# A channel gate over 113 MB: 18 tiles of 64 rows instead of 12 rows and 19 tiles of 60

## The chip, the cores and the metric

One core of one Trainium2 chip. The metric is device time in microseconds (us) of one execution; the profile's span is about 1.4 us shorter than it.

## The reference, cut to what matters

```python
x: (1, 384, 384, 384) bf16, w1d: (1,)
g = jnp.einsum("bhwc->bc", x) / (H * W)      # mean of each channel over all pixels
s = sigmoid(g * w1d[0])                      # one gate per channel
return x * s[:, None, None, :]
```

As 128 partitions see it, x is 1,152 rows of 384 channels per partition. Strictly, everything must be read before anything can be multiplied.

## The kernel before

It reads and writes everything once. It takes a gate `s_early` from the first 4 rows, multiplies by it at once, sums all rows meanwhile, and at the end compares the true gate, in bf16, with the early one. Only if they differ does a second pass run over everything.

The 1,152 rows are a small first tile of 12 and 19 tiles of 60, in four slots of an SBUF arena. For each tile: the load; sums of 44 rows by TensorE (matmuls with ones) and of 16 by VectorE (`reduce_sum`); the gate in place on VectorE; the store. A slot's next load waits for its store to land.

```python
FIRST, EARLY, TILE, SLOTS, BOTH, FORE, OWN = 12, 4, 60, 4, 3, 32, 16
...
    LEAD = EARLY + 4
    load(base, FIRST, 0, hi=LEAD)                       # 8 rows ahead, SyncE's queue
    plan.dma("sync", w_one[0:1, 0:1], w1d.unsqueeze(0), writes=["w_one"])
    for k in range(SLOTS):                              # tiles 0 to 2: half on each queue
        load(slot(k), TILE, row0(k), ("sync", "scalar") if k < BOTH else ("sync",))
        if k == 0:
            load(base, FIRST, 0, ("scalar",), lo=LEAD)  # the other 4 rows
...
    for k in range(n_tiles):                            # steady state
        if k >= SLOTS:
            for i in range(2) if k == SLOTS else () if k < SLOTS + 2 else (k - SLOTS,):
                sum_own(i)                              # VectorE: reduce 16 rows, add
                put(slot(i), TILE, row0(i), ...)        # VectorE: gate; ScalarE: issue store
            if k == SLOTS:
                pause(slot(k))                          # 3 us on ScalarE before load 4
            load(slot(k), TILE, row0(k), ...)
...
    put(slot(last), TILE, row0(last), slot(n_tiles))    # the end
    sum_own(last)
    put(base, FIRST, 0)
    join_own()                                          # VectorE's sums, through TensorE
    add_banks(1, copy=False)                            # TensorE's sums, then the check
```

Of the kernel before, what the change touches and what calls it, by code (L numbers as in the profile page):

```python
# [3 lines left out]
P = 128  # L4
ROW = 384
BF16 = mybir.dt.bfloat16
# [4 lines left out]
ALU = mybir.AluOpType  # L11
# [143 lines left out]
WIDE = 512  # L155



FIRST, EARLY, TILE, SLOTS, BOTH, FORE, OWN = 12, 4, 60, 4, 3, 32, 16


PAUSE = 9


def bass_standalone__channel_attn_eca__vision_kernel(
# [5 lines left out]
    B, H, W, C = x.shape  # L171
# [12 lines left out]
    wrong = nc.alloc_sbuf_tensor("wrong", [P, 1], F32)  # L184
    redo = nc.alloc_sbuf_tensor("redo", [P, 1], I32)
    total = nc.alloc_sbuf_tensor("total", [P, C], F32)
    own = nc.alloc_sbuf_tensor("own", [P, C], F32)
    part = nc.alloc_sbuf_tensor("part", [P, C], F32)
    terms = nc.alloc_sbuf_tensor("terms", [P, 3 * C], BF16)
# [9 lines left out]
    def at(r0, n):  # L199
        assert r0 + n <= n_arena  # L200
        return arena[:, r0 * C : (r0 + n) * C]

    def rows(r0, n):
        return [("sb", r) for r in range(r0, r0 + n)]
# [3 lines left out]
        v, to_v = (at(r, n).rearrange("p (t c) -> p t c", t=n) for r in (place, to))  # L208
        return lambda e: e.tensor_tensor(to_v, v, s_b, ALU.mult)  # L209

    n_tiles = (n_rows - FIRST) // TILE
    base = SLOTS * TILE
    assert (n_rows - FIRST) % TILE == 0 and base + FIRST + 1 + PAUSE <= n_arena
    assert FIRST % 4 == EARLY % 4 == (TILE - OWN) % 4 == 0 and EARLY + 4 < FIRST
    last = n_tiles - 1
    ready = nc.alloc_semaphore("ready")

    def slot(k):
        return k % SLOTS * TILE

    def row0(k):
        return FIRST + k * TILE


    s_true = at(base + FIRST, 1)
    plan = Planner(nc, "a", 70)

    def load(place, n, r0, queues=("sync",), lo=0, hi=None, reads=()):

        i, hi = lo, hi or n  # L230
        for queue, m in zip(queues, split(hi - lo, -(-(hi - lo) // len(queues)))):
            plan.dma(
                queue,
                at(place + i, m),
                dram(x_rows, r0, n)[:, i * C : (i + m) * C],
                reads=reads,
                writes=rows(place + i, m),
            )
            i += m
# [19 lines left out]
    def add_rows(e, group, column, n, start, stop):  # L259

        n_wide = n * C // WIDE
        all_of = [
            mm(
                e,
                acc[group][i % 3][:, :],
                ones[:],
                arena[:, column + i * WIDE : column + (i + 1) * WIDE],
                start and i < 3,
                stop and i >= n_wide - 3,
            )  # L270
            for i in range(n_wide)
        ]
        return all_of[-1]

    def sum_first():
        plan.op(
            "tensor",
            lambda e: add_rows(e, 0, base * C, EARLY, True, True),
            reads=["ones"] + rows(base, EARLY),
            writes=["acc0"],  # L280
        )

    def sum_others():

        def one(e, s):
            e.wait_ge(ready, 1).then_inc(ready, -1)  # L286
            for r, n in ((0, FORE), (FORE, TILE - OWN - FORE)):
                add_rows(e, 1, (slot(s) + r) * C, n, False, False).then_inc(
                    plan.sems["tensor"], 1
                )  # L290

        def emit(e):
            add_rows(e, 1, (base + EARLY) * C, 4, True, False)
            rounds = -(-n_tiles // SLOTS)
            some = n_tiles - (rounds - 1) * SLOTS
            with e.Fori(0, rounds) as k:
                for s in range(some):
                    one(e, s)
                if some < SLOTS:
                    with e.If(k < rounds - 1):  # L300
                        for s in range(some, SLOTS):
                            one(e, s)
            add_rows(
                e, 1, (base + EARLY + 4) * C, FIRST - EARLY - 4, False, True
            ).then_inc(plan.sems["tensor"], 1)

        plan.streams["tensor"].append(("block", emit, None))

# [34 lines left out]
    def join_own():  # L343

        for i in range(3):
            term = terms[:, i * C : (i + 1) * C]
            plan.op(
                "vector",
                lambda e, term=term: e.tensor_copy(term, own[:]),  # L349
                reads=["own"],  # L350
                writes=[f"term{i}"],
            )
            if i < 2:
                plan.op(
                    "vector",
                    lambda e, term=term: e.tensor_tensor(  # L356
                        own[:], own[:], term, ALU.subtract
                    ),
                    reads=["own", f"term{i}"],
                    writes=["own"],  # L360
                )
        for i in range(3):
            term = terms[:, i * C : (i + 1) * C]
            plan.op(
                "tensor",
                lambda e, i=i, term=term: mm(
                    e, acc_own[:, :C], ones[:], term, i == 0, i == 2
                ),
                reads=["ones", f"term{i}"],
                writes=["acc_own"],  # L370
            )
        plan.op(
            "vector",
            lambda e: e.tensor_tensor(total[:], total[:], acc_own[:, :C], ALU.add),  # L374
            reads=["acc_own", "total"],
            writes=["total"],
        )

    def put(place, n, r0, to=None, parts=None):
        to, i = place if to is None else to, 0  # L380
        for m in parts or [n]:
            plan.op(
                "vector",
                gate(to + i, place + i, m, s_early),
                reads=["s_early"] + rows(place + i, m),
                writes=rows(to + i, m),
            )
            i += m
        plan.final.append(
            plan.dma("scalar", dram(o_rows, r0, n), at(to, n), reads=rows(to, n))  # L390
        )

    def pause(r0):

        to = at(base + FIRST + 1, PAUSE)
        plan.op(
            "scalar",
            lambda e: e.activation(  # L398
                to, warm[:, 0:1].broadcast_to([P, PAUSE * C]), ACT_F.Sigmoid
            ),  # L400
            reads=["warm"],
            writes=rows(r0, 1) + ["pause"],
        )
# [26 lines left out]

    plan.op("gpsimd", lambda e: e.memset(warm[:, 0:1], 0.0), writes=["warm"])
    plan.op("vector", lambda e: e.memset(ones[:], 1.0), writes=["ones"])  # L432
    LEAD = EARLY + 4
    load(base, FIRST, 0, hi=LEAD)
    plan.dma("sync", w_one[0:1, 0:1], w1d.unsqueeze(0), writes=["w_one"])
    for k in range(SLOTS):
        load(slot(k), TILE, row0(k), ("sync", "scalar") if k < BOTH else ("sync",))
        if k == 0:
            load(base, FIRST, 0, ("scalar",), lo=LEAD)
    heads = {e: len(plan.streams[e]) for e in ("sync", "scalar")}  # L440
    weight()
    sum_first()
    add_banks(0, copy=True)
    plan.op(
        "scalar",
# [3 lines left out]
        reads=["total", "w_scaled0", "warm1"],  # L449
        writes=["s_early"],  # L450
    )
    plan.need("tensor", rows(base, LEAD))
    sum_others()

    for k in range(n_tiles):
        if k >= SLOTS:

            for i in range(2) if k == SLOTS else () if k < SLOTS + 2 else (k - SLOTS,):
                sum_own(i)
                put(slot(i), TILE, row0(i), parts=None if i else (FORE, TILE - FORE))  # L460
            if k == SLOTS:
                pause(slot(k))
            load(slot(k), TILE, row0(k), reads=["pause"] if k == SLOTS else ())
        there = rows(slot(k), TILE) + (rows(base + LEAD, FIRST - LEAD) if k == 1 else [])
        plan.relay(ready, "gpsimd", "tensor", there, rows(slot(k), FORE), ["acc1"])
        plan.signals("tensor", rows(slot(k) + FORE, TILE - OWN - FORE), ["acc1"])
    plan.signals("tensor", rows(base, FIRST), ["acc1"])
    for k in range(n_tiles - SLOTS, last):
        sum_own(k)
        put(slot(k), TILE, row0(k))  # L470

    put(slot(last), TILE, row0(last), slot(n_tiles))
    sum_own(last)
    put(base, FIRST, 0)
    join_own()


    add_banks(1, copy=False)
    plan.op(
        "scalar",  # L480
        lambda e: e.activation(  # L481
            s_true, total[:], ACT_F.Sigmoid, scale=w_scaled[:, 1:2]
        ),
        reads=["total", "w_scaled1"],
        writes=["s_true"],
    )
    plan.op(
        "vector",
# [19 lines left out]


    again = Planner(nc, "b", 30)  # L510
    half, r0 = base // 2, 0
    for k, n in enumerate(split(n_rows, half)):
        place = k % 2 * half
        again.dma("sync", at(place, n), dram(x_rows, r0, n), writes=rows(place, n))
        again.op(
            "vector",
            gate(place, place, n, s_true),
            reads=rows(place, n),
            writes=rows(place, n),
        )  # L520
        again.final.append(
            again.dma("scalar", dram(o_rows, r0, n), at(place, n), reads=rows(place, n))
        )
        r0 += n
# [93 lines left out]
```

## Time and profile before

| | before |
|---|---|
| median of 6 runs (lowest to highest) | 528.07 us (527.95 to 528.75) |
| span of the profiled run | 526.7 us |
| share of 16 DMA engines' span, both queues | 99.7% |
| VectorE busy | 451 us (86%) |
| TensorE busy | 178 us (34%) |

How to read it: the shares are of one span, so the fullest resource bounds the kernel unless the chain of waits says otherwise. The prediction below goes through both. One thing is added here: three lines of the timeline of the start, with start, duration, engine, operation and, in brackets, the idle time before it with what ended it (ACTq is a transfer that ScalarE issues).

```profile
18.66 9.48 PE L247 MATMUL acc<-arena,ones 128*128 128x512 bf16 x33 [6.64 <-PEq L286]
...
38.57 23.45 ACTq L109 DMA_DIRECT2D out_dram<-arena  x2
...
74.23 3.08 ACT L398 ACTIVATE arena<-warm 128x3456 bf16<-128x3456 f32 x1 [60.11 <-DMA out_dram<-arena]
```

Tile 0's sums start at 18.7 us, the first store is issued at 38.6 (the second at 61.7, in the same merged line), and the first store has landed at 74.2, when the pause begins.

### The profile page before, as it was taken

How to read it: one execution, taken by the hardware profiler on the slowest of the kernel's cores; microseconds unless marked ns; L12 is line 12 of the kernel's file. 1: busy time of each engine (PE TensorE's matmuls, PEld its weight loads, DVE VectorE, ACT ScalarE, POOL GpSimd, SP SyncE). 2: the span in 40 equal slices, each digit the busy share in tenths (PEclk: the TensorE clock that was granted, in tenths of full speed). 3: DMA queues.
4: the chain of work that ended last, by engine and by line, in shares of the span. 5: the costliest groups of instructions: out<-in, count | busy, mean ns of one | idle time of the engine just before them, and what ended most of it. 6: DMA issues, size and time to landing. Idle time of an engine off the chain costs nothing.

```text
span 526.7 us, 905 instructions
## 1 busy us (share of the span) xinstructions
PE 178.2 (34%) x640; PEld 0.2 (0%) x2; DVE 451.1 (86%) x82; ACT 5.8 (1%) x5; POOL 0.3 (0%) x5
## 2 busy tenths in 40 slices
PE   2534660060606051414233241515060606060701
PEld 0000000000000000000000000000000000000000
DVE  1899999999796969796969696979697979889796
ACT  1000020000000000000000000000000000000000
POOL 0000000000000000000000000000000000000000
PEclk9978877576766767675858585858585858576765
DMA  9999999999999999999999999999999999999998
GB/s 387 430 422 460 406 448 395 444 448 448 395 444 448 448 395 444 448 441 402 444 448 434 409 445 444 434 413 441 448 430 416 441 444 434 416 441 444 430 420 367
DMA packets 6340, 226.51 MB, mean 430 GB/s; under 512 B 706, under 2 KB 706, under 8 KB 962
## 3 DMA queue, kind: packets, MB, share of 16 engines
q10 hardware_dynamic: 3456, 122.49, 53.8%
q1 hardware_dynamic: 2882, 104.01, 45.9%
q14 instruction: 2, 0.02, 0.0%
HBM read 113.25 MB, written 113.25 MB: 430 GB/s over the span
## 4 chain that ended last, share of the span: by engine, by line
DMA 64%; DVE 27%; issue 4%; PE 2%; ACT 0%; DVEq 0%
DMA out_dram<-arena 33%; DMA arena<-in_x_dram 31%; DVE arena L209 13%; DVE part L331 12%; PE acc L247 1%; DVE own L338 1%; DVE total L319 0%; DVE own L356 0%; DVE terms L349 0%; ACT arena L481 0%; DVE total L489 0%; DVE total L374 0%; DVE wrong L497 0%; PE acc_own L247 0%; DVE redo L503 0%
## 5 line engine op out<-in xcount | busy, mean ns | idle before, releaser
L247 PE MATMUL acc<-arena,ones 128*128 128x512 bf16 x635 | 176.3, 447 | 314.0 <-PEq L286 314.0
L209 DVE TENSOR_TENSOR arena<-arena,s_early 128x23040 bf16<-128x23040 bf16 (+3 forms) x21 | 233.5, 11123 | 5.2 <-DMA arena<-in_x_dram 4.0
L331 DVE TENSOR_REDUCE part<-arena 128x384 f32<-128x6144 bf16 x18 | 189.5, 10526 | 53.4 <-DMA arena<-in_x_dram 53.4
L331 DVE TENSOR_REDUCE own<-arena 128x384 f32<-128x6144 bf16 x1 | 10.5, 10495 | 1.1 <-DMA arena<-in_x_dram 1.1
L338 DVE TENSOR_TENSOR own<-own,part 128x384 f32<-128x384 f32 x18 | 10.0, 558 | 0.6
L247 PE MATMUL acc_own<-terms,ones 128*128 128x384 bf16 x3 | 1.4, 478 | 16.8 <-DVE terms L349 16.8
L424 DVE TENSOR_SCALAR w_scaled<-w_all 128x1 f32<-128x1 f32 x2 | 0.2, 152 | 7.9 <-PE w_all L415 7.9
L481 ACT ACTIVATE arena<-total,w_scaled 128x384 bf16<-128x384 f32 x1 | 0.6, 614 | 444.3 <-DVE total L319 444.3
L319 DVE TENSOR_TENSOR total<-total,acc 128x128 f32<-128x128 f32 (+2 forms) x11 | 4.5, 408 | 0.4
L398 ACT ACTIVATE arena<-warm 128x3456 bf16<-128x3456 f32 x1 | 3.1, 3082 | 60.1 <-DMA out_dram<-arena 60.1
L415 PE MATMUL w_all<-w_one,ones 1*128 1x1 bf16 x1 | 0.2, 159 | 9.2 <-DMA w_one<-in_w1d_dram 9.2
L317 DVE COPY total<-acc 128x384 f32<-128x384 f32 x1 | 0.6, 558 | 1.2 <-PE acc L247 1.2
L409 ACT ACT_TABLE_LOAD x1 | 1.3, 1283 | 2.8 <-issue 2.8
L432 DVE MEMSET ones<- 128x128 bf16 x1 | 0.2, 165 | 1.3 <-PEq L603 1.3
L356 DVE TENSOR_TENSOR own<-own,terms 128x384 f32<-128x384 f32 x2 | 1.1, 559 | 0.1
L489 DVE TENSOR_TENSOR total<-arena,s_early 128x384 f32<-128x384 uint16 x1 | 0.6, 559 | 0.7 <-ACT arena L481 0.7
L349 DVE CAST terms<-own 128x384 bf16<-128x384 f32 x3 | 1.1, 357 | 0.1
L374 DVE TENSOR_TENSOR total<-total,acc_own 128x384 f32<-128x384 f32 x1 | 0.6, 556 | 0.6 <-PE acc_own L247 0.6
L446 ACT ACTIVATE s_early<-total,w_scaled 128x384 bf16<-128x384 f32 x1 | 0.6, 614 | 9.2 <-DVE total L319 9.2
L245 PE MATMUL acc<-arena,ones 128*128 128x512 bf16 x1 | 0.6, 608 | 0.0
L497 DVE TENSOR_REDUCE wrong<-total 128x1 f32<-128x384 f32 x1 | 0.6, 553 | 0.0
L409 ACT ACTIVATE warm<-warm 128x1 f32<-128x1 f32 x1 | 0.2, 202 | 0.0
(8 smaller groups left out, 0.9 us busy)
## 6 DMA issues: line engine op xcount, KB each, us to landing
out_dram<-arena ACTq DMA_DIRECT2D x19, 5760.0 KB, 44.7
arena<-in_x_dram SPq DMA_DIRECT2D x16, 5760.0 KB, 40.9
arena<-in_x_dram ACTq DMA_DIRECT2D x3, 2880.0 KB, 34.5
arena<-in_x_dram SPq DMA_DIRECT2D x3, 2880.0 KB, 29.0
out_dram<-arena ACTq DMA_DIRECT2D x1, 1152.0 KB, 11.1
arena<-in_x_dram SPq DMA_DIRECT2D x1, 768.0 KB, 7.7
arena<-in_x_dram ACTq DMA_DIRECT2D x1, 384.0 KB, 21.2
w_one<-in_w1d_dram SPq DMA_DIRECT2D x1, 0.0 KB
```

The costliest lines, as they stand in the source:

```text
L209: return lambda e: e.tensor_tensor(to_v, v, s_b, ALU.mult)
L245: loaded.append(e.matmul(bank, weights, moving, start=start, stop=stop))
L247: return e.add_instruction(mybir.InstMatmult(name=nc.get_next_instruction_name(), engine=mybir.EngineType.PE, ins=[e.lower_ap(moving), e.l ...
L317: emit = lambda e, part=part, of=of: e.tensor_copy(part, of)
L319: emit = lambda e, part=part, of=of: e.tensor_tensor(part, part, of, ALU.add)
L331: lambda e: e.reduce_sum(to[:], view, axis=mybir.AxisListType.X),
L338: lambda e: e.tensor_tensor(own[:], own[:], part[:], ALU.add),
L349: lambda e, term=term: e.tensor_copy(term, own[:]),
L356: lambda e, term=term: e.tensor_tensor(own[:], own[:], term, ALU.subtract),
L374: lambda e: e.tensor_tensor(total[:], total[:], acc_own[:, :C], ALU.add),
L398: lambda e: e.activation(to, warm[:, 0:1].broadcast_to([P, PAUSE * C]), ACT_F.Sigmoid),
L409: lambda e: e.activation(warm[:, 1:2], warm[:, 0:1], ACT_F.Sigmoid),
```

## The change

The intent: no small first tile, fewer and larger transfers, nothing left to gate after the last tile, and a last addition that waits less for TensorE. The first 8 rows of tile 0 are loaded ahead and the early gate comes from its first 4. Since the tiles are larger, the loads of the start are dealt out anew: tile 1 whole on SyncE's queue, tile 2 on ScalarE's.

```diff
-FIRST, EARLY, TILE, SLOTS, BOTH, FORE, OWN = 12, 4, 60, 4, 3, 32, 16
+TILE, SLOTS, EARLY, LEAD, FORE, OWN = 64, 4, 4, 8, 32, 16
...
-    load(base, FIRST, 0, hi=LEAD)
+    load(0, TILE, 0, hi=LEAD)
     plan.dma("sync", w_one[0:1, 0:1], w1d.unsqueeze(0), writes=["w_one"])
-    for k in range(SLOTS):
-        load(slot(k), TILE, row0(k), ("sync", "scalar") if k < BOTH else ("sync",))
-        if k == 0:
-            load(base, FIRST, 0, ("scalar",), lo=LEAD)
+    load(0, TILE, 0, ("sync", "scalar"), lo=LEAD)
+    load(slot(1), TILE, row0(1))
+
+    load(slot(2), TILE, row0(2), ("scalar", "scalar"))
+    load(slot(3), TILE, row0(3))
...
     put(slot(last), TILE, row0(last), slot(n_tiles))
     sum_own(last)
-    put(base, FIRST, 0)
     join_own()                  # without its last addition
-    add_banks(1, copy=False)
+    add_banks(1, copy=True)
+    ... total += acc_own        # the addition, now after the banks
```

Cut: TensorE's sums open and close with matmuls over a column of zeros, since no small tile is there to do it; the true gate goes to a row of the last slot; the second pass has smaller pieces.

More of the change, by code (lines that the diff above doesn't have):

```diff
@@ L186, in bass_standalone__channel_attn_eca__vision_kernel @@
     total = nc.alloc_sbuf_tensor("total", [P, C], F32)
+    zeros = nc.alloc_sbuf_tensor("zeros", [P, 2], BF16)
     own = nc.alloc_sbuf_tensor("own", [P, C], F32)
@@ L209, in gate @@
         return lambda e: e.tensor_tensor(to_v, v, s_b, ALU.mult)
-    n_tiles = (n_rows - FIRST) // TILE
+    n_tiles = n_rows // TILE
     base = SLOTS * TILE
-    assert (n_rows - FIRST) % TILE == 0 and base + FIRST + 1 + PAUSE <= n_arena
-    assert FIRST % 4 == EARLY % 4 == (TILE - OWN) % 4 == 0 and EARLY + 4 < FIRST
+    assert n_rows % TILE == 0 and base + PAUSE <= n_arena
+    assert EARLY % 4 == FORE % 4 == (TILE - OWN) % 4 == 0 and EARLY <= LEAD <= FORE
     last = n_tiles - 1
@@ L221, in row0 @@
     def row0(k):
-        return FIRST + k * TILE
-    s_true = at(base + FIRST, 1)
+        return k * TILE
+    s_true = at(slot(last), 1)
     plan = Planner(nc, "a", 70)
@@ L273, in add_rows, with sum_early, nothing, sum_all @@
         return all_of[-1]
-    def sum_first():
+    def sum_early():
         plan.op(
             "tensor",
-            lambda e: add_rows(e, 0, base * C, EARLY, True, True),
-            reads=["ones"] + rows(base, EARLY),
+            lambda e: add_rows(e, 0, 0, EARLY, True, True),
+            reads=["ones"] + rows(0, EARLY),
             writes=["acc0"],
         )
-    def sum_others():
+    def nothing(e, bank, start):
+        none = zeros[:, 0:1].broadcast_to([P, WIDE])
+        return mm(e, acc[1][bank][:, :], ones[:], none, start, not start)
+    def sum_all():
         def one(e, s):
@@ L292, in emit @@
         def emit(e):
-            add_rows(e, 1, (base + EARLY) * C, 4, True, False)
+            for i in range(3):
+                nothing(e, i, True)
             rounds = -(-n_tiles // SLOTS)
@@ L302, in emit @@
                             one(e, s)
-            add_rows(
-                e, 1, (base + EARLY + 4) * C, FIRST - EARLY - 4, False, True
-            ).then_inc(plan.sems["tensor"], 1)
+            for i in range(3):
+                done = nothing(e, i, False)
+            done.then_inc(plan.sems["tensor"], 1)
         plan.streams["tensor"].append(("block", emit, None))
@@ L371, in join_own @@
             )
-        plan.op(
-            "vector",
-            lambda e: e.tensor_tensor(total[:], total[:], acc_own[:, :C], ALU.add),
-            reads=["acc_own", "total"],
-            writes=["total"],
-        )
     def put(place, n, r0, to=None, parts=None):
@@ L393, in pause @@
     def pause(r0):
-        to = at(base + FIRST + 1, PAUSE)
+        to = at(base, PAUSE)
         plan.op(
@@ L432, in bass_standalone__channel_attn_eca__vision_kernel @@
     plan.op("vector", lambda e: e.memset(ones[:], 1.0), writes=["ones"])
-    LEAD = EARLY + 4
-    load(base, FIRST, 0, hi=LEAD)
+    plan.op("gpsimd", lambda e: e.memset(zeros[:], 0.0), writes=["zeros"])
+    load(0, TILE, 0, hi=LEAD)
     plan.dma("sync", w_one[0:1, 0:1], w1d.unsqueeze(0), writes=["w_one"])
-    for k in range(SLOTS):
-        load(slot(k), TILE, row0(k), ("sync", "scalar") if k < BOTH else ("sync",))
-        if k == 0:
-            load(base, FIRST, 0, ("scalar",), lo=LEAD)
+    load(0, TILE, 0, ("sync", "scalar"), lo=LEAD)
+    load(slot(1), TILE, row0(1))
+    load(slot(2), TILE, row0(2), ("scalar", "scalar"))
+    load(slot(3), TILE, row0(3))
     heads = {e: len(plan.streams[e]) for e in ("sync", "scalar")}
     weight()
-    sum_first()
+    sum_early()
     add_banks(0, copy=True)
@@ L451, in bass_standalone__channel_attn_eca__vision_kernel @@
     )
-    plan.need("tensor", rows(base, LEAD))
-    sum_others()
+    plan.need("tensor", ["zeros"])
+    sum_all()
     for k in range(n_tiles):
@@ L463, in bass_standalone__channel_attn_eca__vision_kernel @@
             load(slot(k), TILE, row0(k), reads=["pause"] if k == SLOTS else ())
-        there = rows(slot(k), TILE) + (rows(base + LEAD, FIRST - LEAD) if k == 1 else [])
+        there = rows(slot(k), TILE)
         plan.relay(ready, "gpsimd", "tensor", there, rows(slot(k), FORE), ["acc1"])
         plan.signals("tensor", rows(slot(k) + FORE, TILE - OWN - FORE), ["acc1"])
-    plan.signals("tensor", rows(base, FIRST), ["acc1"])
+    plan.signals("tensor", [], ["acc1"])
     for k in range(n_tiles - SLOTS, last):
@@ L473, in bass_standalone__channel_attn_eca__vision_kernel @@
     sum_own(last)
-    put(base, FIRST, 0)
     join_own()
-    add_banks(1, copy=False)
+    add_banks(1, copy=True)
+    plan.op(
+        "vector",
+        lambda e: e.tensor_tensor(total[:], total[:], acc_own[:, :C], ALU.add),
+        reads=["acc_own", "total"],
+        writes=["total"],
+    )
     plan.op(
@@ L484, in bass_standalone__channel_attn_eca__vision_kernel @@
         reads=["total", "w_scaled1"],
-        writes=["s_true"],
+        writes=["s_true"] + rows(slot(last), 1),
     )
@@ L510, in bass_standalone__channel_attn_eca__vision_kernel @@
     again = Planner(nc, "b", 30)
-    half, r0 = base // 2, 0
+    above = slot(last) + 1
+    half, r0 = (base - above) // 2, 0
     for k, n in enumerate(split(n_rows, half)):
-        place = k % 2 * half
+        place = above + k % 2 * half
         again.dma("sync", at(place, n), dram(x_rows, r0, n), writes=rows(place, n))
```

## The prediction

> **What bounds the kernel now.** I read the engines' busy line first, then the DMA slices and queues. VectorE looks like the bound (86%), so the reader has to hold it against the DMA engines before believing it.
>
> ```profile
> PE 178.2 (34%) x640; PEld 0.2 (0%) x2; DVE 451.1 (86%) x82; ACT 5.8 (1%) x5; POOL 0.3 (0%) x5
> ...
> DMA  9999999999999999999999999999999999999998
> ...
> DMA packets 6340, 226.51 MB, mean 430 GB/s; under 512 B 706, under 2 KB 706, under 8 KB 962
> ## 3 DMA queue, kind: packets, MB, share of 16 engines
> q10 hardware_dynamic: 3456, 122.49, 53.8%
> q1 hardware_dynamic: 2882, 104.01, 45.9%
> ```
>
> The two queues' packets fill 53.8 + 45.9 = 99.7% of what 16 engines have in the span of 526.7 us, so 525 us each: no hole worth the name. q1 is SyncE's queue (loads), q10 ScalarE's (stores and some early loads). The GB/s line jumps between 395 and 460, but the busy line does not follow it down: packets are long (next part) and I take the dips for the way whole packets are counted into slices, not for lost time. That is a choice of mine.
>
> Next the chain of waits, because a chain that goes through every buffer could also set the pace.
>
> ```profile
> 404.47 44.67 DMA out_dram<-arena
> ...
> 449.15 40.79 DMA arena<-in_x_dram
> ...
> 489.97 12.16 DVE arena L209
> 502.13 10.34 DVE part L331
> ...
> 513.05 2.47 DVE arena L209
> ...
> 523.48 0.15 DVE redo L503
> ```
>
> A slot's life is load 40.8 + reduce, add and gate 23.2 + store 44.7 us, 109 us for four slots, so 27.2 us a tile. But a tile is 2 x 5.9 MB, and at 433 GB/s (what the stretch from 120 to 485 us moves) that is 27.2 us of transfer as well. So the chain is long because transfers queue: a load alone would need 5.9 MB / 433 GB/s = 13.6 us, not 40.8. VectorE has 23.2 us of work per 27.2 us. The bound is the transfer of 226.5 MB; the chain's length is its consequence.
>
> Last, the two ends, where a change of tiling could act:
>
> ```profile
> core 0: us, PE busy (x) PEld busy (x) DVE busy (x) ACT busy (x) POOL busy (x), PEclk, DMA share, GB/s
> 120.00:485.00 365.00, 118.26 (x429) 0.00 (x0) 311.87 (x40) 0.00 (x0) 0.00 (x0) 0.69 1.00 433
> ...
> 515.00:525.30 10.30, 1.43 (x3) 0.00 (x0) 6.97 (x16) 0.61 (x1) 0.00 (x0) 0.50 0.93 401
> 525.30:526.70 1.40, 0.00 (x0) 0.00 (x0) 0.00 (x0) 0.00 (x0) 0.00 (x0) 0.50 0.09 39
> ```
>
> In the packet records the first big packet starts at 1.0 us and the last ends at 526.3 us. What is not transfer is about 1 us of start and 1 us of engines finishing unevenly. The check of the gate ends at 523.6 us (the last line of the chain) and its flag is read by 524.5 us, before the last store lands: it is hidden by 2 us.
>
> **What the Trainium skill says.** "DMA: Bandwidth & Descriptors", section "Specifications", puts the ceiling of 16 engines at 435 GB/s and a core's HBM share at about 358. This trace agrees with the first (433 in the steady stretch, read and write together) and goes over the second, so no HBM limit shows here. The same page, "Queues, rings and completion order", says that an engine goes round-robin between queues packet by packet. The trace agrees: with 23,040-byte packets on both queues each has about 8 of the 16 engines at 22 to 26 us; when SyncE's are 23,040 and ScalarE's 3,072 bytes (14 to 20 us), SyncE's has over 13. I use this for the start. The same page, "Latency and other measured facts", warns of row pitches in HBM of large powers of two, where a copy fell to half rate and a few KiB of padding restored it. A pitch of 64 rows is 48 KB, three times a power of two, where 60 rows are 45 KB; no run so far shows whether that matters.
>
> **The change part by part.**
>
> 1. Bytes: 113.25 MB in and 113.25 MB out, unchanged.
>
> 2. Packets. One packet is one partition's contiguous piece: 46,080 bytes take 1.702 us and 23,040 bytes 0.855 us (medians of the packet records). The difference gives 0.0368 us per 1,000 bytes and 1.702 - 2 x 0.847 = 0.008 us fixed per packet. Before: 5,632 data packets. After: 128 x (7 in the initial loads + 14 later loads + 18 stores) = 4,992. Saved 640 x 0.008 / 16 = **0.3 us**. A 49,152-byte packet should take 0.008 + 1.807 = 1.815 us.
>
> 3. VectorE. Removed: one reduce (10.5), one add (0.6), the 12-row gate's 2.6 us; gates grow by 64/60 in all but cover the same rows. So 451 - 12 = about 439 us busy. None of it is on the bound: 24.1 us of work per tile against 2 x 6.29 MB / 433 GB/s = 29.05 us. Worth 0.
>
> 4. TensorE. 36 matmuls a tile instead of 33 (the last group before has 36 and takes 9.9 us), under the 10.5 us reduce beside it. The six matmuls over a column of zeros only open and close the sums. Worth 0.
>
> 5. The end. After the last load: gate 12.15 x 64/60 = 13.0, reduce and add 10.9, splitting into terms 2.2, banks 2.8 (the matmuls of the terms now run beside them), last add, sigmoid, compare and flag 2.6 + 0.9: 32.4 us against 34.5 before. The 12-row gate's 2.5 us and a wait of 0.5 go, 0.8 comes. Stores still outstanding when the last load lands: the end of the last but two, then two whole tiles of 14.5 us each at one queue's full rate (8 x 1.815), so at least 29 us plus up to one more tile. The last store is issued 13 us after the last load, while the one before it still has work: no hole. By part 6 the phase leaves some 39 us of stores, over 32.4. Worth 0: the check was and stays hidden.
>
> 6. The start, where the order of loads really changes. Per engine each load is 8 packets. Before: tile 1 is split over both queues; after: it is whole on SyncE's queue with 49,152-byte packets, and tile 2 is on ScalarE's with 24,576. Alternating packets from the trace's sizes: the 8 rows ahead land near 7.5 us as now; tile 0's halves (21,504 bytes, 0.80 us) at about 13 and 21 us (before: 14.6 and 18.7, as ScalarE's tiny 4-row packets let SyncE's half run ahead; they are gone). So TensorE's sums of tile 0's first 32 rows end near 28.5 us instead of 26.2, and the first store goes out near 41.4 instead of 38.6. Tile 1 (8 pairs of 1.815 + 0.911) lands near 43 instead of about 30; VectorE then idles 2 us and issues the store of tile 1 near 67 (before 62.0). ScalarE's loads end at 51, SyncE's last initial load near 69; the first store lands near 75 (+1.8 of latency; the same arithmetic for the kernel before gives 72.4 against a measured 74.2). Then only the store of tile 1 has packets until the load of tile 4 arrives after the pause, near 79. It was issued 8 us before it is needed, so the engines stay full. **Worth 0**, but the margin falls from 12 us to 8.
>
> 7. The end's raggedness is that of 16 engines with equal work; packets of 1.8 us at the end instead of 0.35 could add up to 0.5 us.
>
> Sum: -0.3 from packets, +0.2 for raggedness, 0 elsewhere: 528.05 - 0.1 to -0.3, I say **527.8 us**.
>
> **The rivals.**
>
> A. *The check at the end comes out.* If the reader takes the chain at its word, VectorE ends it, and 34.5 - 32.4 = 2 us less after the last load would give 526. Against: the last packets end at 526.3, 2 us after the flag is read. I give it little.
>
> B. *A hole opens at the start.* Tile 1 lands 13 us later, and if the two queues share otherwise than packet by packet, the store of tile 1 misses the end of the first store while the next load still sits behind the pause. Each us of miss is a us of all 16 engines: 2 to 5 us, so 530 to 533. For it: that is the only stretch with a single store at work (70 to 80 us in the trace). Against: the 8 us margin.
>
> C. *The 48 KB pitch slows transfers.* One per cent longer packets cost 5.2 us. For it: only the page's warning. Against: at 45 KB the rate is already the engines' own.
>
> D. *Larger tiles take away a periodic loss.* If the GB/s dips were real, 19 rounds becoming 18 might win 1 to 2%. Against: the 99.7%.
>
> **Range and chances.** Three runs of the kernel before spread over 0.7 us. A and D pull down by 1 to 3 us, B and C up by 2 to 5, each unlikely: 526.3 to 529.6. Two per cent are 10.6 us, which none of A or B reaches: faster 0.01, within 2% 0.96, slower 0.03 (C).
>
> **What would show it.** The two queues should still fill over 99.4% of 16 engines; 49,152-byte packets should take 1.81 to 1.82 us (C: more); the slices from 60 to 90 us should stay at full DMA share (B: a slice under 0.9); VectorE's busy time should fall to about 439 us with no gain in time; the flag should be read at least 2 us before the last store lands. The prediction is wrong if the DMA share has a hole, or if the profile shows the packets themselves changed.

## The result, and the profile after

| | before | after |
|---|---|---|
| median of 6 runs each | 528.07 us | 527.96 us |
| lowest to highest | 527.95 to 528.75 | 527.94 to 528.25 |
| span of the profiled run | 526.7 us | 526.5 us |
| data packets | 5,632 | 4,992 |
| packet time per DMA engine (packet records) | 524.7 us | 524.6 us |
| last packet ends | 526.3 us | 525.9 us |

The ratio is 0.9996, 95% interval 0.9983 to 1.0009: the same. Ratios here are the mean time of one kernel's fast runs over that of the other's of the same rounds, so not quite the ratio of the medians quoted.

The page of the changed kernel, the lines that answer to those in the prediction:

```profile
PE 180.0 (34%) x648; PEld 0.2 (0%) x2; DVE 440.0 (84%) x78; ACT 5.8 (1%) x5; POOL 0.3 (0%) x6
...
DMA packets 5620, 226.51 MB, mean 430 GB/s; under 512 B 626, under 2 KB 626, under 8 KB 754
...
q10 hardware_dynamic: 3024, 122.29, 53.7%
q1 hardware_dynamic: 2594, 104.20, 46.0%
```

VectorE lost 11 us of work and the time did not follow. The queues still fill 99.7% of 16 engines, with the same bytes at the same mean rate.

The end, in the chain of waits (start, duration, what):

```profile
489.92 12.96 DVE arena L210
502.88 10.34 DVE part L338
...
521.28 0.15 DVE redo L510
```

The last load lands at the same time as before (489.9 us), the check is done 2.2 us earlier (before: 523.5 + 0.15), and the stores go on to 525.9: the earlier check has nothing to give.

The start, in the timeline:

```profile
22.77 10.78 PE L248 MATMUL acc<-arena,ones 128*128 128x512 bf16 x36 [10.66 <-PEq L292]
...
44.14 24.76 ACTq L109 DMA_DIRECT2D out_dram<-arena  x2
...
76.09 3.08 ACT L399 ACTIVATE arena<-warm 128x3456 bf16<-128x3456 f32 x1 [61.87 <-DMA out_dram<-arena]
```

The first store is issued 5.6 us later than before, the store of tile 1 at 68.6 us (before 61.7), and yet the first store lands only 1.9 us later. Did the engines stay full? Here are two windows of the changed kernel, of 5 and of 16 us. The columns are window and length, busy time and instructions of TensorE, its weight loads, VectorE, ScalarE and GpSimd, the granted clock, the DMA share and GB/s.

```profile
70.00:75.00 5.00, 2.72 (x7) 0.00 (x0) 5.00 (x1) 0.00 (x0) 0.00 (x0) 0.50 0.79 344
...
66.00:82.00 16.00, 9.67 (x35) 0.00 (x0) 15.97 (x4) 3.08 (x1) 0.00 (x0) 0.68 1.02 442
```

The first line looks like a hole. It is none: in the packet records 16.0 of 16 engines are at work in every 2 us from 70 to 82 us. Whole packets of 1.8 us are counted into windows, and neighbouring windows show 1.09. The second line, long against a packet, is the one to believe.

### The profile page after: what moved, and what is told of

Read it like the earlier page. It is cut to its first block, busy times and chain, and to the rows that moved or that the text cites. A ratio compares the mean times of both kernels' runs of the same rounds, so it can differ in the third digit from the quotient of the medians.

```text
span 526.5 us, 902 instructions
## 1 busy us (share of the span) xinstructions
PE 180.0 (34%) x648; PEld 0.2 (0%) x2; DVE 440.0 (84%) x78; ACT 5.8 (1%) x5; POOL 0.3 (0%) x6
## 4 chain that ended last, share of the span: by engine, by line
DMA 42%; another core or an unknown queue 27%; DVE 21%; issue 7%; SPq 0%; ACT 0%; DVEq 0%
DMA arena<-in_x_dram 24%; DMA out_dram<-arena 18%; DVE part L338 12%; DVE arena L210 7%; DVE own L345 1%; DVE total L326 0%; SPq L109 0%; DVE own L363 0%; DVE terms L356 0%; ACT arena L488 0%; DVE total L496 0%; DVE total L482 0%; DVE wrong L504 0%; DVE total L324 0%
## 5 line engine op out<-in xcount | busy, mean ns | idle before, releaser
L210 DVE TENSOR_TENSOR arena<-arena,s_early 128x24576 bf16<-128x24576 bf16 (+1 forms) x19 | 233.2, 12278 | 11.5 <-PE acc L248 6.5
L338 DVE TENSOR_REDUCE part<-arena 128x384 f32<-128x6144 bf16 x17 | 179.2, 10539 | 56.9 <-DMA arena<-in_x_dram 56.9
L338 DVE TENSOR_REDUCE own<-arena 128x384 f32<-128x6144 bf16 x1 | 10.4, 10435 | 0.6 <-DMA arena<-in_x_dram 0.6
L248 PE MATMUL acc<-zeros,ones 128*128 128x512 bf16 x6 | 2.3, 507 | 0.0
```

The source lines that it names most:

```text
L210: return lambda e: e.tensor_tensor(to_v, v, s_b, ALU.mult)
L248: return e.add_instruction(mybir.InstMatmult(name=nc.get_next_instruction_name(), engine=mybir.EngineType.PE, ins=[e.lower_ap(moving), e.l ...
L338: lambda e: e.reduce_sum(to[:], view, axis=mybir.AxisListType.X),
```

## The experiments

Each is the changed kernel with one edit, unless said otherwise. The question of the first five is whether transfer alone sets the time and how well the rest is hidden.

### More work for VectorE

```diff
-TILE, SLOTS, EARLY, LEAD, FORE, OWN = 64, 4, 4, 8, 32, 16
+TILE, SLOTS, EARLY, LEAD, FORE, OWN = 64, 4, 4, 8, 32, 20
```

> VectorE sums 20 rows of each tile instead of 16: some 2.6 us more per tile (10.5 x 20/16 = 13.1), 18 x 2.6 = 47 us more VectorE work in all, about 487 us busy, 26.7 us per tile against 29.05 us of transfer. Theory (the transfer of 226.5 MB alone sets the time): no change against the changed kernel, within 0.5 us, 527.9 us. Rival (VectorE, or the chain through the four slots, sets the pace): each round of four slots is at least 2.6 us longer, 18/4 x 2.6 = 12 us, so 540 us; if VectorE itself is the bound, +47 us.

Measured: 528.68 us median of 4 (528.37 to 530.57), ratio to the kernel before 1.0004 (0.9987 to 1.0020). VectorE's line on its page:

```profile
PE 170.6 (32%) x598; PEld 0.2 (0%) x2; DVE 485.3 (92%) x78; ACT 5.8 (1%) x5; POOL 0.3 (0%) x6
```

45 us more work on what looks like the fullest engine cost under 1 us. Neither VectorE nor the chain through the slots sets the pace.

### Fewer bytes (wrong on purpose)

```diff
-            plan.dma("scalar", dram(o_rows, r0, n), at(to, n), reads=rows(to, n))
+            plan.dma("scalar", dram(o_rows, r0, n)[:, : 60 * C], at(to, 60), reads=rows(to, n))
```

> Wrong on purpose: every store writes 60 of its 64 rows, the rest is as before, VectorE too. 18 x 4 x 128 x 768 bytes = 7.08 MB less. Theory: 7.08 MB x 0.0368 us per 1,000 bytes / 16 = 16.3 us less, 511.7 us. Rival (VectorE or reads or the chain of waits for VectorE set the pace): little or no change, 525 to 528 us.

Measured: 512.35 us median of 5 (511.61 to 516.18), ratio 0.9693. The output is wrong, as intended. 7.08 MB less gave 15.6 us less where 16.3 were worked out: bytes are the price.

### Smaller packets

Every load and store of a whole tile goes as four of 16 rows on the same queue.

```diff
-    load(slot(1), TILE, row0(1))
+    load(slot(1), TILE, row0(1), ("sync",) * 4)
...
-            load(slot(k), TILE, row0(k), reads=...)
+            load(slot(k), TILE, row0(k), ("sync",) * 4, reads=...)
```

> Every load and store of 64 rows in four of 16 rows (tile 0's loads as they are): 12,288-byte packets instead of 49,152, 13,312 more packets. Theory: 0.008 us fixed per packet, 13,312 x 0.008 / 16 = 6.7 us more of packet time per engine, plus a little for four times as many completion writes: 534.6 to 536 us; one packet takes 0.460 us. Rival (the fixed part is hidden, only bytes count): 528 us. Rival (small packets cost far more): over 540 us.

Measured: 533.13 us median of 4 (533.07 to 534.63), ratio 1.0094. A 12,288-byte packet takes 0.460 us (median), as worked out. 5.2 us for 13,312 packets are 5.2 x 16 / 13,312 = 0.006 us a packet. So the prediction's 0.008 was a little high, and the 640 packets that the change saves are worth 0.2 to 0.3 us: real, and under the noise.

### Three slots

```diff
-TILE, SLOTS, EARLY, LEAD, FORE, OWN = 64, 4, 4, 8, 32, 16
+TILE, SLOTS, EARLY, LEAD, FORE, OWN = 64, 3, 4, 8, 32, 16
-    load(slot(3), TILE, row0(3))
```

> Three slots of 64 rows instead of four. If the chain through the slots set the pace (109 us for four tiles before, 116 now), each tile would cost 4/3 of it: about 700 us. Theory (transfers queue, the chain stretches to fill): 24 us of VectorE, some 6 us of issue and landing, and 58 us of load and store at half rate each are 88 us a round against 3 x 29.05 = 87 us of transfer: nearly hidden, 528 to 540 us.

Measured: 551.4 us median of 4 (550.1 to 557.2), ratio 1.047. A miss: worse than I expected, though far from 700. The busy line of its DMA engines shows one loss:

```profile
DMA  9999399999999999999999999999999999999995
```

There is a hole near 65 us (8.8 us per engine in the packet records), since no fourth tile is there to load while the first store is awaited. At the end the check comes out: the last packet ends 5.0 us before the span does (0.6 us in the changed kernel). Four slots are needed, but for the start and a few tight places, not for the pace. The rest only made sense later (below): four clusters of some 40 long load packets, each costing 1.4 to 1.9 us per engine.

### A longer check

```diff
 # in sum_own(k), before own += part
+        if k == last:
+            plan.op("vector", lambda e: e.reduce_sum(part[:], view, axis=...), ...)
```

> The last tile's reduce is run twice (10.4 us more between the last load and the flag). In the changed kernel the flag is read by 522.6 us and the last packet ends at 525.9 us, the span at 526.5. Theory: the check is hidden by some 3.5 us, so the flag comes at 533.0 and the time grows by 10.4 - 3.5 to 4 = 6.5 to 7 us, to 534.6 us. Rival A (the check already ends the kernel): +10.4 us, 538.4. A rival in which stores after it are the end by far: no change.

Measured: 535.85 us median of 4 (535.78 to 535.97). That is 7.9 us more for 10.4 us of work, so the check was hidden by 2.5 us, not by 3.5: after the flag the program takes another 1.3 us to end, which I had left out. Its end, in windows:

```profile
515.00:526.40 11.40, 0.96 (x2) 0.00 (x0) 11.23 (x6) 0.00 (x0) 0.00 (x0) 0.50 0.83 358
526.40:534.50 8.10, 0.48 (x1) 0.00 (x0) 4.65 (x12) 0.61 (x1) 0.00 (x0) 0.50 0.00 0
```

Now 8.1 us pass without a byte moved: this is what a check that bounds the kernel looks like. Rival A is out for the changed kernel. The same 2.5 us also just cover the longer reduce of the first experiment.

### A late store at the start

The same edit with `k == 1` in place of `k == last`.

> The reduce of tile 1 is run twice, so its store is issued 10.5 us later, at 79 us instead of 68.5. In the changed kernel the first store lands at 76.1 us and only the store of tile 1 is there to follow it until the load of tile 4 has packets at 82 us. Theory: the margin is 7.6 us less some 1 to 2 us from issue to first packet; the engines stand empty for about 4 to 6 us near 76 to 81 us and the time grows by as much, to 532 to 534 us, with nothing won back later. Rival (there is slack in the later rounds which takes up a late start): no change, 528. Rival (the slot chain sets the pace): +10.5 us, 538.5.

Measured: 536.37 us median of 4 (533.93 to 539.47), ratio 1.0171 (1.0131 to 1.0210). The window that was 442 GB/s above:

```profile
66.00:82.00 16.00, 8.43 (x31) 0.00 (x0) 16.00 (x2) 2.91 (x1) 0.00 (x0) 0.64 0.80 344
```

The hole is there (4.0 us per engine in the packet records) and nothing wins it back. So rival B's mechanism exists; the change simply stays clear of it. But the median lost 8 us, not 4 to 6, and the runs disagree by 5.5 us. Something else was at work: even in the profiled run, the fastest (533.93), the mean packet time per engine is 2.0 us longer than in the changed kernel (526.6 against 524.6), most of it between 84 and 88 us, as the load of tile 4 joins the store. Hole and longer packets together are the 6.0 us of that run.

### The order of loads as before

```diff
-    load(slot(1), TILE, row0(1))
-    load(slot(2), TILE, row0(2), ("scalar", "scalar"))
+    load(slot(1), TILE, row0(1), ("sync", "scalar"))
+    load(slot(2), TILE, row0(2), ("sync", "scalar"))
```

> The changed kernel with the loads of tiles 1 and 2 split over both queues as before. Theory: the start costs nothing and the engines are full in both orders: 527.9 us within 0.3, while the store of tile 1 is issued some 5 us earlier than 68.5. Rival (the new order loses at the start what the new tail wins, and the two cancel): 1 to 3 us faster, 525 to 527 us.

Measured: 534.08 us median of 4 (532.75 to 536.71), ratio 1.0124 (1.0094 to 1.0154). My theory said 527.9: it falls here. There is no hole: all 16 engines have a packet at all times. But the packets last longer. Windows from 40 to 100 us, first of the changed kernel, then of this one:

```profile
40.00:100.00 60.00, 27.48 (x105) 0.00 (x0) 59.55 (x8) 3.08 (x1) 0.00 (x0) 0.73 1.00 426
```

```profile
40.00:100.00 60.00, 24.32 (x99) 0.00 (x0) 59.93 (x8) 3.08 (x1) 0.00 (x0) 0.73 1.01 410
```

Full share, fewer bytes. From 100 to 480 us both move 434 GB/s. In the packet records the mean packet time per engine is 527.5 us against 524.6, nearly all of the excess between 44 and 95 us. That is 2.9 of the 4.8 us by which this profiled run (532.75) is longer; for the rest the engines finish less evenly (the last store lands on the 16 over 5.6 us instead of 1.5).

What is different there? ScalarE's queue runs out of loads at 42 us, and the first store, issued at 42.0, begins at about 46 us: just when SyncE's queue begins the load of tile 3. In the changed kernel that load is about five packets ahead on each engine when the store begins. My second theory: **a load and a store of whole tiles that start in step, within about a packet of each other, lengthen each other's packets.** The three-slot run fits it by the times of issue: its four clusters of long packets begin at 215, 304, 393 and 481 us, and there a load and a store were issued at 214.1 and 216.1, 303.1 and 304.6, 392.2 and 393.6, 481.8 and 483.1. The later pairs 3 us or more apart show 0.1 us or less. One pair does not fit so neatly: right after the hole, a store issued at 68.2 and a load issued at 71.7 us also saw 1.4 us per engine of long packets. And by the packet records the run does not tell the cases apart: in all four clusters the store's first packets begin 5 to 6 us, three packets, after the load's, but so they do in the pair that begins at 129 us, which shows under 0.1 us of it. What "in step" has to mean is therefore open.

### Tests of the second theory

**Old order, shifted.** Tile 0's last 4 rows as a small load of their own on ScalarE's queue, which moves the first store back by several packets:

```diff
-    load(0, TILE, 0, ("sync", "scalar"), lo=LEAD)
+    load(0, TILE, 0, ("sync",), lo=LEAD, hi=36)
+    load(0, TILE, 0, ("scalar",), lo=36, hi=60)
+    load(0, TILE, 0, ("scalar",), lo=60)
```

> The loads split over both queues as in old_order (534.1 us), but tile 0's last 4 rows go as a small load of their own on ScalarE's queue, as the kernel before had it: 8 small packets more per engine on that queue, so the first store no longer starts in the same packet round as the load of tile 3 but some 4 packets later. First idea (a load and a store of whole tiles that start in step lengthen each other's packets): long packets between 44 and 95 us fall from 3.5 us per engine to about the 0.6 of the changed kernel, time 528 to 529. Rival (splitting tiles 1 and 2 over both queues is itself what costs): 533 to 535 us again.

Measured: 527.88, 528.33, 532.27 and 533.14 us. The profiled run (527.88) has no long clusters and moves 433 GB/s from 40 to 100 us. The theory's part holds in that run, but two of the four runs are 4 to 5 us longer all the same, and they have no packet records.

**Reduce of tile 0 twice** (the same edit with `k == 0`):

> The changed kernel with the reduce of tile 0 run twice: the first store is issued near 54.6 us, some 4 us after ScalarE's queue has run dry, but out of step with the load of tile 3 (about 6 of its 8 packets done). Idea in step: no long packets near 55 to 65 us. Rival (a store that arrives at a dry queue lengthens packets): some 0.6 us per engine or more there. Later the store of tile 1 (issued near 79) comes about with the load of tile 4 (near 79.5): a hole of 2 to 5 us near 75 and, if in step matters, long packets from 80 to 95 us. Time 531 to 537.

A miss in its making: VectorE had been waiting 6.5 us for TensorE there, so the added reduce was mostly hidden, the first store still found ScalarE's queue busy, and neither case came about. Measured 529.46 us median of 4 (528.46 to 532.02). It taught something else: in the profiled run (532.02) the mean packet time is an ordinary 524.8 us, but the last packet ends at 530.2, while nearly all other engines are done by 526. One engine is late.

**The kernel before, with its 12 first rows in one load**:

```diff
-    LEAD = EARLY + 4
+    LEAD = FIRST
...
-        if k == 0:
-            load(base, FIRST, 0, ("scalar",), lo=LEAD)
```

> The kernel before, with the 12 first rows in one load on SyncE's queue instead of 8 there and 4 on ScalarE's: ScalarE's queue then ends its loads near 42 us and the first store starts about together with the load of tile 3, with 60-row tiles (46,080-byte packets, 45 KB apart). If starting in step is enough, the same lengthening as in old_order: 531 to 536 us. If it needs the 48 KB pitch or the 6 MiB tiles: no long packets, 528 us.

Inconclusive. The first store began about 6 us, three packets, after the load of tile 3, so the two were not in step, and the runs are 527.67, 528.78, 535.46 and, in the slow state, 537.47 us. Whether it takes a 48 KB pitch to lengthen packets is open.

**All four tiles split**, so that the first store starts after the loads of both queues:

```diff
-    load(slot(1), TILE, row0(1))
-    load(slot(2), TILE, row0(2), ("scalar", "scalar"))
-    load(slot(3), TILE, row0(3))
+    load(slot(1), TILE, row0(1), ("sync", "scalar"))
+    load(slot(2), TILE, row0(2), ("sync", "scalar"))
+    load(slot(3), TILE, row0(3), ("sync", "scalar"))
```

> All of the first four tiles split over both queues: the loads of both queues end together near 57 us and the first store then runs with no load beside it until the load of tile 4. Idea in step (old_order lost its 6 us because the first store and the load of tile 3 started within a packet of each other): no long packets between 44 and 75 us, 528 to 529.5 us. Rival (splitting tiles 1 and 2 over both queues is what costs): 533 us or more.

Measured: 528.76 and 528.79 us in two runs, 531.83 to 532.45 in four. The profiled run (532.45) has no long clusters: splitting is not what lengthens packets. Its mean packet time is 524.6 us, as in the changed kernel. Nearly all engines are done by 525.5 us, and the last packet ends at 530.6: one late engine again. It falls behind by degrees: in the landings it is 2.1 us behind the median engine at 114 us, 5.0 at 233 and 5.9 at the end.

**In step on purpose**, with the new order otherwise:

```diff
-    load(slot(2), TILE, row0(2), ("scalar", "scalar"))
+    load(slot(2), TILE, row0(2), ("scalar", "sync"))
```

> The changed kernel, only the second half of tile 2 goes on SyncE's queue instead of ScalarE's: tile 1 stays whole, ScalarE's queue is empty early, and the first store (issued near 44 us) starts within about a packet of the load of tile 3 (near 45). Idea in step: long packets of 2 us or more per engine between 45 and 95 us, 531 to 536 us. Rival (splitting tile 1 is what costs, or the old order as such): 528 us.

Measured: 533.59 us median of 4 (532.82 to 534.14), ratio 1.0095 (1.0079 to 1.0112), all four of them long. Its window:

```profile
40.00:100.00 60.00, 26.08 (x105) 0.00 (x0) 59.93 (x8) 3.08 (x1) 0.00 (x0) 0.73 1.01 402
```

| packets of 49,152 bytes that start from 44 to 95 us | number | over 1.915 us (usual: 1.815) | mean |
|---|---|---|---|
| changed kernel | 417 | 16 | 1.837 us |
| old order | 414 | 104 | 1.949 us |
| in step on purpose | 402 | 152 | 1.996 us |

One half tile moved to the other queue costs 5.6 us, with the lengthening where the theory put it. Of the 6.2 us by which the profiled run (534.14) is longer, 4.1 are longer packets (mean packet time 528.7 us); the rest is again an uneven finish. Together with the other three profiles this supports the second theory: where the load of tile 3 is at most one packet ahead of the first store (old order, in step on purpose) these packets cost 3.5 and 4.6 us per engine from 44 to 95 us, and where it is three or more ahead or already over (the changed kernel and the other profiles of these tests) 0.1 to 1.0.

Three things keep it from being shown. The theory does not cover all of the lengthening: 0.8 of the old order's 3.5 us per engine, and 1.0 of the 4.6 us in the last run, come after 84 us, beside a load that starts 11 us after its store. A rival is untested: in both long orders the first store also met a queue of ScalarE that had run empty, and the reduce of tile 0 twice, meant to part the two, did not. (The kernel before with its first rows in one load had an empty queue too and only 1.0 us of long packets, but with 60-row tiles.) And the mechanism below is not settled: packet number n of a load and of a store concerns the same partitions, which may matter, but no run tests it. Nor is it known why single engines come late in some executions of some orders.

No correct version beat both kernels. The profiled spans of the two are within 2 us of their own packet time, and those 2 us are all that scheduling could still win.

## Why the prediction was right, point by point

- **The bound** (transfer, not VectorE, not the chain). Shown: more VectorE work cost under 1 us, fewer bytes gave 15.6 us.
- **Parts 1 and 2.** 4,992 packets as counted, and the 49,152-byte packet takes 1.815 us as worked out. The saving in packet time was 0.13 us rather than 0.3, since the early small packets took longer. With 1.815 us at a pitch of 48 KB, **rival C** is out in the steady state, which moves 434 GB/s against 433.
- **Part 3.** 440 us busy against the 439 worked out. The sum was loose: its items add up to 13.7 us, it took off 12, and 11 went, since the gated rows are the same in both kernels and only the reduce and the add go. **Part 4.** TensorE stayed hidden, except at the first gate, which now waits 6.5 us for it instead of 1.3.
- **Part 5.** The flag is read by 522.6 us, 3.3 us ahead of the last packet's end. Stores went on for 36 us after the last load, not 39. The true margin is 2.5 us.
- **Part 6** was right in its times: the first store landed at 76.1 us (worked out: 75 + 1.8), the store of tile 1 was issued at 68.6 (67), the margin was 7.5 us (8). The first store was issued 2.7 us later than I had it, because tile 0's halves and TensorE took longer. But its verdict on the order of loads, "Worth 0", was the step that failed. It holds for this pair of kernels, not for the part alone: with 64-row tiles, the small first load gone and tiles 1 and 2 split as before, the kernel takes 534.1 us, and the new order takes those 6 us away. So the sum near zero hides one part that costs and one that takes the cost back. I had looked for holes alone, and a full engine with longer packets is no hole. That the new order stays clear of this was luck: nothing in the prediction looked for it.
- **Part 7.** No raggedness was added: the last packet ends 0.4 us earlier.
- **Rival D.** The dips in GB/s came to nothing, as supposed: with 12,288-byte packets the line is nearly flat (most slices 428 to 433). One of my own tests was built on the same sand: "B: a slice under 0.9" would have called the 5 us window at 0.79 a hole.

## What to carry to other kernels

When the DMA engines are full end to end, count bytes and packets first: work taken from other engines, and a shorter tail, are worth nothing until they stick out. Change the parts one at a time even when the sum is zero, for here larger tiles without the small first load cost 6 us under the old order of loads, and a new order in the same change took that back. And look at the length of packets as well as at holes: a window with full share and fewer GB/s, long against one packet, gives it away.

## What the Trainium skill lacked or had wrong

- No page has it that the packets of whole-tile loads and stores on two queues can lengthen while all 16 engines stay busy: 1.996 us on average instead of 1.837 from 44 to 95 us, 402 against 426 GB/s from 40 to 100 us, and 5.6 us of the kernel's time, an uneven finish included. That it is the start in step is supported by four profiles, with the gaps said above; the mechanism is open.
- No page has it that on SyncE's and ScalarE's queues one of the 16 engines can come some 5 us late in some executions of a kernel and not in others (528.8 or 531.8 to 532.5 us with all tiles split; in the profiled run of 532.45 the last packet at 530.6 us, most engines done by 525.5). "DMA: Bandwidth & Descriptors", section "Latency and other measured facts", has engines 7 and 15 as usually slower and guesses at GpSimd's path; no transfer here is GpSimd's, and the records do not name the engine.
- "DMA: Bandwidth & Descriptors", section "Where 436 GB/s comes from", says that for transfers between HBM and SBUF the HBM side, about 358 GB/s, binds. With one core at work both kernels moved 433 to 434 GB/s in the steady state, half read and half written. The sentence needs the condition that the page gives earlier, in its section on measured bandwidth: about 358 GB/s each is for both cores of a pair streaming.
